# Holding later batches' attention behind the MLP tiles, and moving the first loads to a second DMA queue

## The chip, the cores and the metric

The kernel runs on one core of one Trainium2 chip. The metric is the device time of one execution in microseconds. One execution was taken by the hardware profiler; all times inside the kernel come from that one. The engines are TensorE (PE, with PEld for its weight loads), VectorE (DVE), ScalarE (ACT), GpSimd (POOL) and SyncE (SP), which issues DMAs. Each engine works through its own instructions in the order in which the program has them, and waits at the head of its queue.

## The reference

Eight batches of 512 tokens `x` and 32 state rows `state`, 8 heads of 64. Attention runs both ways between them, and every row of the result passes an MLP with a squared ReLU:

```python
scores  = scale * x @ state.T        # per batch and head
xread   = softmax(scores)  @ state   # 512 rows
sread   = softmax(scale * state @ x.T) @ x   # 32 rows
attn    = concat([xread, sread])     # 8 * 544 = 4352 rows of 512
h       = attn @ w_in                # 512 -> 2048
out     = (relu(h) ** 2) @ w_out     # 2048 -> 512
```

`w_in` and `w_out` come as 64-bit floats.

## The kernel before

**Arithmetic.** Most products are made from a high and a low part (`split`, L96: ScalarE rounds to the high part at L97, VectorE or GpSimd subtracts it at L98 for the low part). So one product is three matmuls: high by high, low by high, high by low. The 64-bit weights arrive as pairs of 32-bit words and `singles` (L100) turns them into 32-bit floats: one ScalarE operation (L108) and three VectorE operations (L109, L113, L117).

**z.** The token rows never get `xread` as such. The state of each head is multiplied into `w_in` first, which gives z (`z_part`, L148, products pz), written to DRAM as `zd` and fetched for each batch by `z_fetch`. zs[0] serves batches 0 to 3, zs[1] batches 4 to 7. `z_state` (L127) loads and splits the state for it.

**Attention of a batch** (`attention`, `attention_group`, two groups p and q of four heads). Steps: `pad` (L242, loads a batch's state as sp_raw), `load_t` (x transposed, xt_raw), `cut_t` (split), `scores` (pst in batches 0 and 1; two halves pq added into st from batch 2 on), `soft1` and `soft1b` (the softmax over the state rows: L315 maximum, L316 subtraction, L317 exponential, L322 sum, L324 reciprocal, L325 product, L327 transpose into `at`, then split into a_hi and a_lo). The subtraction and the product run on GpSimd in batches 0 to 2. The state's own reads come three batches later: `load_n`, `cut_n` (xn_hl), `turn` (L338 to L340 scale e, then transposes pt into e_hl) and `read` (products pr).

**MLP tiles** (`mlp`, L372). A tile is one batch with 128 of the 2048 hidden columns. `up` makes ph from z and a (L392, six matmuls), then relu (L394, ScalarE), square (L396 on ScalarE for the first ten tiles, L398 on VectorE afterwards) and the split into g_hi and g_lo. `down` (L418, twelve matmuls into four po) follows two tiles later. The tiles run in this order: batch 0 with column blocks 0 to 5, batch 1 with 0 to 9, batch 0 with 6 to 15, batch 1 with 10 to 15, then batches 2 to 7 with all sixteen each. So batch 1 starts with the seventh tile, and batch 2 with tile 32 counted from 0. After a batch's last block, L599 adds po to the sums.

**What sets the order.** `mlp` calls `aux` twice for each tile, a slot each. `aux` asks two lists of class `Ahead` for steps: `weights` (loading and converting w_in and w_out, making z) and `reads` (attention of batches 1 and on, and the reads). Each list spreads its steps evenly up to a due slot, and holds a step back until its `begin`. For batch b's attention the list is due one slot ahead of the batch's first tile; from batch 2 on it begins when batch b − 2 has ended: slot 52 for batch 2, due at slot 63. That is the order in which the program writes its instructions. Behind it a scheduler orders each engine's instructions by a timing model of its own and by dependencies, and may pull an instruction far ahead of where it was written.

Loads of weights, and some others, share four buffers (tag `raw`), and are freed by the conversion. The loads were all issued by SP; the stores of z (`zd`, L217) by ScalarE.

Of the kernel before, what the change touches and what calls it, by code (L numbers as in the profile page):

```python
# [9 lines left out]
F32 = mybir.dt.float32  # L10
# [8 lines left out]
def memory_attention_then_relu2_ffn(  # L19
# [71 lines left out]
    zd, st, z_first = {}, {}, []  # L91
# [2 lines left out]
            zd[G, k] = dr.tile([P, NG, HG, FW], F32, name=f"zd_{G}_{k}")  # L94

    def split(hi, lo, src, eng_lo):  # L96
        nc.scalar.copy(out=hi, in_=src)  # L97
        eng_lo.tensor_sub(out=lo, in0=src, in1=hi.bitcast(F32))  # L98

    def singles(out_f, words):  # L100

        low, high = words[..., 0], words[..., 1]
        bits = out_f.bitcast(I32)
        nc.scalar.activation(out_f, high.bitcast(F32), AF.Abs, scale=2.0**-112)  # L108
        nc.vector.tensor_scalar(  # L109
            out=bits, in0=bits, scalar1=3, scalar2=0x7FFFFFF8,  # L110
            op0=ALU.logical_shift_left, op1=ALU.bitwise_and,
        )
        nc.vector.scalar_tensor_tensor(  # L113
            out=bits, in0=high, scalar=-0x80000000, in1=bits,
            op0=ALU.bitwise_and, op1=ALU.bitwise_or,
        )
        nc.vector.scalar_tensor_tensor(  # L117
            out=bits, in0=low, scalar=29, in1=bits,
            op0=ALU.logical_shift_right, op1=ALU.bitwise_or,
        )  # L120


    def z_state(G):
        if G == 0:
            raw = sb.tile([P, H, GB * N], F32, name="st_f", tag="x_hl", bufs=1)
            st["raw"] = raw
        else:  # L127
            raw = sb.tile([P, H, GB * N], F32, name="st_raw", tag="raw", bufs=RAW)
        for j in range(2):
            nc.sync.dma_start(out=raw[j * D:(j + 1) * D].rearrange("d h m -> d (h m)"), in_=stT[G])  # L130
        hi = sb.tile([P, H, GB * N], F32R, name="stz_hi", bufs=1)
        lo = sb.tile([P, H, GB * N], F32R, name="stz_lo", bufs=1)
        if G:
            split(hi, lo, raw, nc.gpsimd)
        else:
            for i in range(2):
                own = slice(i * D, (i + 1) * D)
                other = slice((1 - i) * D, (2 - i) * D)
                for v in (hi, lo):
                    nc.gpsimd.memset(v[other, i::2, :].bitcast(F32), 0.0)  # L140
                split(hi[own, i::2, :], lo[own, i::2, :], raw[own, i::2, :], nc.vector)
        st[G] = hi, lo

    def z_part(G, k, g):
# [5 lines left out]
        def load():  # L150
            if G:
                box["wf"] = sb.tile([P, nq, FW], F32, name="wf", bufs=2)
                nc.sync.dma_start(out=box["wf"], in_=wd[k][:, ccs, :])
                return
            raw = sb.tile([P, nq, FW, 2], I32, name="w_raw", tag="raw", bufs=RAW)
            nc.sync.dma_start(out=raw.rearrange("p c f w -> p (c f w)"), in_=w_in[k * NG + g])
            box["raw"] = raw

        def convert():
            wf = sb.tile([P, nq, FW], F32, name="wf", bufs=2)  # L160
            singles(wf, box["raw"])
            nc.sync.dma_start(out=wd[k][:, ccs, :], in_=wf)
            box["wf"] = wf

# [52 lines left out]
                nc.scalar.dma_start(out=dst, in_=stage)  # L217
            return run

        return load, convert, cut, [product(i) for i in range(2)]  # L220

    def z_fetch(b, k):
        if k or b:
# [157 lines left out]
    def mlp(width, fcs, first, rows, aux):  # L381
# [6 lines left out]
        def up(fc):  # L388
# [10 lines left out]
            units[0] += 1  # L399
            hi = sb.tile([P, S], F32R, name="g_hi", bufs=2)[:, :width]  # L400
            lo = sb.tile([P, S], F32R, name="g_lo", bufs=2)[:, :width]
            split(hi, lo, ph, nc.vector)
            gs[fc] = hi, lo

        def down(i):
# [65 lines left out]
    def emit(step):  # L471
        step()
        emitted[step] = slot[0]

    class Ahead:

        def __init__(self):
            self.steps, self.due, self.done = [], [], 0  # L480

        def add(self, steps, due, begin=0):
            self.steps += [(begin, s_) for s_ in steps]
# [23 lines left out]
    for b in range(B):
        for g in range(NG):
# [169 lines left out]
```

## Time and profile before

| | us |
|---|---|
| three timed runs, median (lowest to highest) | 708.6 (707.11 to 710.06) |
| the profiled execution's own time | 708.43 |
| its span, first to last instruction | 706.6 |
| mean granted TensorE clock | 0.973 of full speed |
| TensorE busy | 669.8 |
| VectorE busy | 452.2 |
| ScalarE busy | 398.3 |
| GpSimd busy | 199.3 |

The profile has several views. The page gives busy shares, forty slices of the span in tenths, and the chain of work that ended last. A table of stretches gives each engine's busy time in a stretch, the granted clock and the DMA share. Groups of instructions by line give count, busy time and mean duration, and what ended the idle time before them. The timeline gives single instructions with their start, duration and, in brackets, the idle time of the engine before them and its releaser. Names like po<-wo_hi,g_hi say what is written from what. Matmuls are pipelined, so the distance between two starts is the time that one takes from the engine, not its shown duration.

### The profile page before, as it was taken

The numbers are of one execution on the slowest core, as the hardware profiler recorded it, in microseconds if no ns is written. First come the engines' busy times: TensorE is split into PE (matmuls) and PEld (weight loads), VectorE is DVE, ScalarE is ACT, GpSimd is POOL, SyncE is SP. The second block draws the span as 40 slices with busy tenths as digits, with TensorE's granted clock in tenths as the row PEclk, the third lists the DMA queues.
The fourth block names the chain that finished last, engine by engine and source line by source line (L and its number), as shares of the span: only waits on it lengthen the run. The fifth ranks groups of instructions, "written<-read, shape, count | busy, mean of one in ns | idle before, by whom it ended". The sixth has DMA issues, their size and how long they took to land.

```text
span 706.6 us, 9753 instructions
## 1 busy us (share of the span) xinstructions
PE 669.8 (95%) x3152; PEld 551.6 (78%) x3152; DVE 452.2 (64%) x757; ACT 398.3 (56%) x727; POOL 199.3 (28%) x181
## 2 busy tenths in 40 slices
PE   4688789999999999999999999999999999999997
PEld 2355668778888888888888878888888888888996
DVE  4859999758456944447945794797944445443553
ACT  3767687567565863467735653665654344332442
POOL 2314433345443540053403240344242022000000
PEclk8589999999999999999999999999999999999999
DMA  8898899435363542344423312412241112100421
GB/s 276 270 315 283 258 306 315 131 97 153 98 202 122 166 149 62 102 135 120 135 78 120 87 48 74 139 58 90 89 150 61 30 31 90 31 16 0 130 80 32
DMA packets 74548, 90.58 MB, mean 128 GB/s; under 512 B 7680, under 2 KB 57600, under 8 KB 74496
## 3 DMA queue, kind: packets, MB, share of 16 engines
q1 hardware_dynamic: 56896, 72.90, 32.9%
q10 hardware_dynamic: 17600, 17.04, 7.1%
q8 instruction: 25, 0.41, 0.3%
q14 instruction: 27, 0.22, 0.1%
HBM read 60.03 MB, written 29.88 MB: 127 GB/s over the span
## 4 chain that ended last, share of the span: by engine, by line
PE 79%; DVE 8%; DMA 6%; issue 2%; ACT 2%; SPq 1%; POOL 0%; DVEq 0%; ACTq 0%; POOLq 0%
PE po L418 47%; PE ph L392 25%; PE pz L203 3%; DMA wo_raw<-w_out 2%; PE pr L355 2%; DMA sp_raw<-stP 2%; PE pq L288 1%; PE pt L343 1%; DVE wf L117 1%; DVE wf L113 1%; DVE z_lo L98 1%; DVE g_lo L98 1%; DMA zd<-z_stage 1%; DMA xt_raw<-xT 1%; DVE wf L109 1%
## 5 line engine op out<-in xcount | busy, mean ns | idle before, releaser
L418 PE MATMUL po<-wo_hi,g_hi 128*128 128x512 f32 x544 | 217.3, 400 | 0.6 <-ACT g_hi L97 0.5
L418 PE MATMUL po<-wo_lo,g_hi 128*128 128x512 f32 x544 | 215.0, 395 | 0.0
L398 DVE TENSOR_TENSOR ph<-ph,r 128x512 f32<-128x512 f32 (+1 forms) x134 | 89.1, 665 | 169.1 <-ACT r L394 168.9
L394 ACT ACTIVATE r<-ph 128x512 f32<-128x512 f32 (+1 forms) x144 | 82.1, 572 | 171.0 <-PE ph L392 169.6
L418 PE MATMUL po<-wo_hi,g_lo 128*128 128x512 f32 x544 | 152.2, 392 | 0.0
L418 PEld LDWEIGHTS po<-wo_hi,g_hi 128*128 128x128 f32 x544 | 103.9, 191 | 22.4 <-ACT g_hi L97 2.0
L418 PEld LDWEIGHTS po<-wo_lo,g_hi 128*128 128x128 f32 x544 | 103.9, 191 | 19.5
L418 PEld LDWEIGHTS po<-wo_hi,g_lo 128*128 128x128 f32 x544 | 101.5, 189 | 21.1 <-issue 1.0
L98 DVE TENSOR_TENSOR g_lo<-ph,g_hi 128x512 fp32r<-128x512 f32 (+1 forms) x144 | 94.4, 656 | 36.3 <-ACT g_hi L97 27.7
L97 ACT CAST g_hi<-ph 128x512 fp32r<-128x512 f32 (+1 forms) x144 | 81.0, 563 | 57.9 <-DVE ph L398 51.7
L392 PE MATMUL ph<-a_hi,z_hi 128*128 128x512 f32 x256 | 81.4, 399 | 2.6 <-DVE nm L306 1.5
L392 PE MATMUL ph<-a_lo,z_hi 128*128 128x512 f32 x256 | 80.1, 392 | 0.0
L392 PE MATMUL ph<-a_hi,z_lo 128*128 128x512 f32 x256 | 80.0, 394 | 0.0
L98 POOL TENSOR_TENSOR xn_hl<-xn_raw,xn_hl 128x1024 fp32r<-128x1024 f32 x16 | 38.9, 2432 | 138.0 <-ACT xn_hl L97 71.2
L182 POOL TENSOR_TENSOR w<-wf,w 64x512 fp32r<-64x512 f32 x32 | 43.0, 1343 | 74.9 <-ACT w L181 69.8
L392 PEld LDWEIGHTS ph<-a_hi,z_hi 128*128 128x128 f32 x256 | 47.6, 190 | 15.2 <-DVE g_lo L98 2.1
L392 PEld LDWEIGHTS ph<-a_hi,z_lo 128*128 128x128 f32 x256 | 48.5, 190 | 10.4
L392 PEld LDWEIGHTS ph<-a_lo,z_hi 128*128 128x128 f32 x256 | 48.2, 189 | 10.5 <-issue 0.3
L98 POOL TENSOR_TENSOR xt_hl<-xt_raw,xt_hl 128x1024 fp32r<-128x1024 f32 x12 | 28.9, 2406 | 75.4 <-ACT xt_hl L97 43.7
L98 DVE TENSOR_TENSOR z_lo<-z_raw,z_hi 128x512 fp32r<-128x512 f32 x64 | 47.9, 750 | 0.3 <-DMA wd<-wf 0.3
L97 ACT CAST z_hi<-z_raw 128x512 fp32r<-128x512 f32 x64 | 39.2, 615 | 1.3 <-DMA wd<-wf 0.8
L98 POOL TENSOR_TENSOR wo_lo<-wof,wo_hi 128x512 fp32r<-128x512 f32 x16 | 25.2, 1578 | 51.4 <-ACT wo_hi L97 51.4
(97 smaller groups left out, 833.7 us busy)
## 6 DMA issues: line engine op xcount, KB each, us to landing
zd<-z_stage ACTq DMA_DIRECT2D x64, 256.0 KB, 3.2
z_raw<-zd SPq DMA_DIRECT2D x252, 64.0 KB, 2.4
xt_raw<-xT SPq DMA_DIRECT2D x16, 512.0 KB, 3.8
w_raw<-w_in SPq DMA_DIRECT2D x16, 512.0 KB, 5.3
wo_raw<-w_out SPq DMA_DIRECT2D x16, 512.0 KB, 5.8
xn_raw<-xn SPq DMA_DIRECT2D x16, 512.0 KB, 3.9
out<-sum SPq DMA_DIRECT2D x32, 256.0 KB, 2.5
wd<-wf SPq DMA_DIRECT2D x16, 256.0 KB, 3.7
```

Source lines behind the costliest of these rows:

```text
L97: nc.scalar.copy(out=hi, in_=src)
L98: eng_lo.tensor_sub(out=lo, in0=src, in1=hi.bitcast(F32))
L109: nc.vector.tensor_scalar(out=bits, in0=bits, scalar1=3, scalar2=0x7FFFFFF8, op0=ALU.logical_shift_left, op1=ALU.bitwise_and,)
L113: nc.vector.scalar_tensor_tensor(out=bits, in0=high, scalar=-0x80000000, in1=bits, op0=ALU.bitwise_and, op1=ALU.bitwise_or,)
L117: nc.vector.scalar_tensor_tensor(out=bits, in0=low, scalar=29, in1=bits, op0=ALU.logical_shift_right, op1=ALU.bitwise_or,)
L182: nc.gpsimd.tensor_sub(out=w[other], in0=wf[own], in1=w[own].bitcast(F32))
L203: nc.tensor.matmul(pz[:, q, :], lhsT=a[:, h, :], rhs=w, start=j == 0, stop=j == len(todo) - 1,)
L355: nc.tensor.matmul(pr[:, q].rearrange("p i c -> p (i c)"), lhsT=my["e"][:, t, q].rearrange("p i n -> p (i n)"), rhs=my["xn"][:, t, q].rear ...
L392: nc.tensor.matmul(ph, lhsT=w, rhs=v, start=i == 0, stop=i == len(todo) - 1)
L394: nc.scalar.activation(r, ph, AF.Relu)
L398: nc.vector.tensor_mul(out=ph, in0=ph, in1=r)
L418: nc.tensor.matmul(po[t], lhsT=g, rhs=w, start=i == 0 and j == 0, stop=i == last and j == 2)
```

## The change

Four things change.

1. `mark` remembers, for each engine, the last of certain instructions: the two of the split of each tile's g, and the loads of weights on SP. The list `reads` is made with `behind=True`: each of its steps is written inside `behind_marks`, which forbids the scheduler to put any of the step's instructions on an engine ahead of that engine's remembered instruction. TensorE and GpSimd have no mark. The list `weights` stays free.
2. The first two halves of `w_in` (k = 0) are requested from ScalarE's queue instead of SP's.
3. The state's load for zs[0] goes to ScalarE's queue too, and each half of the partitions loads only the heads that it uses (half the bytes). Loading and splitting are two steps now, and the splitting is held behind the conversion of the second half of w_in.
4. `stT` keeps its dimension of heads on the way in. Arithmetic and amounts of work are otherwise the same.

```diff
+    def mark(*those):
+        for i in those:
+            marks[i.ins.engine] = i.ins
+
+    def behind_marks():
+        stack = ExitStack()
+        for i in marks.values():
+            stack.enter_context(tc.issue_after(i))
+        return stack
...
         for j in range(2):
-            nc.sync.dma_start(out=raw[j * D:(j + 1) * D].rearrange("d h m -> d (h m)"), in_=stT[G])
+            rows = slice(j * D, (j + 1) * D)
+            if G:
+                nc.sync.dma_start(out=raw[rows], in_=stT[G])
+            else:
+                nc.scalar.dma_start(out=raw[rows, j::2, :], in_=stT[G, :, j::2, :])
...
-            nc.sync.dma_start(out=raw.rearrange("p c f w -> p (c f w)"), in_=w_in[k * NG + g])
+
+            queue = nc.scalar if k == 0 else nc.sync
+            load = queue.dma_start(out=raw.rearrange("p c f w -> p (c f w)"), in_=w_in[k * NG + g])
+            if k:
+                mark(load)
...
-            split(hi, lo, ph, nc.vector)
+            mark(*split(hi, lo, ph, nc.vector))
...
         def next(self):
-            emit(self.steps[self.done][1])
+            with behind_marks() if self.behind else ExitStack():
+                emit(self.steps[self.done][1])
...
-        q["cut_t"], q["scores"], q["soft1"], p["soft1b"], q["soft1b"], lambda: z_state(0),
+        q["cut_t"], q["scores"], q["soft1"], p["soft1b"], q["soft1b"], lambda: z_state_load(0),
...
-    weights, reads = Ahead(), Ahead()
+    with tc.issue_after(z0[1][4]["done"].ins):
+        z_state_cut(0)
+
+    weights, reads = Ahead(), Ahead(behind=True)
```

The load in `wo_load` is marked as well. The orders of the engines move as follows. First VectorE just ahead of the seventh tile's g_lo, in the kernel before:

```order
L98 TENSOR_TENSOR w_1_865<-wf,w_0_864 128x512
L113 SCALAR_TENSOR_TENSOR wf<-w_raw,wf 128x512
L109 TENSOR_SCALAR wof<-wof 128x512
L117 SCALAR_TENSOR_TENSOR wf<-w_raw,wf 128x512
L113 SCALAR_TENSOR_TENSOR wof<-wo_raw,wof 128x512
L117 SCALAR_TENSOR_TENSOR wof<-wo_raw,wof 128x512
L98 TENSOR_TENSOR z_lo<-z_raw,z_hi 128x512
L98 TENSOR_TENSOR w_1_985<-wf,w_0_984 128x512
L109 TENSOR_SCALAR wf<-wf 128x512
L113 SCALAR_TENSOR_TENSOR wf<-w_raw,wf 128x512
L117 SCALAR_TENSOR_TENSOR wf<-w_raw,wf 128x512
L98 TENSOR_TENSOR g_lo<-ph,g_hi 128x512
```

and in the changed kernel (wf is a half block of w_in, wof a block of w_out, w_1 the low part of a wf for z):

```order
L98 TENSOR_TENSOR w_1_1267<-wf,w_0_1266 128x512
L127 SCALAR_TENSOR_TENSOR wf<-w_raw,wf 128x512
L98 TENSOR_TENSOR z_lo<-z_raw,z_hi 128x512
L131 SCALAR_TENSOR_TENSOR wf<-w_raw,wf 128x512
L123 TENSOR_SCALAR wof<-wof 128x512
L127 SCALAR_TENSOR_TENSOR wof<-wo_raw,wof 128x512
L131 SCALAR_TENSOR_TENSOR wof<-wo_raw,wof 128x512
L98 TENSOR_TENSOR w_1_1359<-wf,w_0_1358 128x512
L98 TENSOR_TENSOR g_lo<-ph,g_hi 128x512
```

The last low part of w_in ahead of the seventh g_lo was w_1_985; now two later halves (1113 and 1267) and the last, 1359, stand ahead of it, with more conversions of w_out.

Then TensorE where batch 2 begins. ph_1944 is the up product of its first tile, a_hi_1686 its attention; po0_1759 to po3_1762 are batch 1's sums. Before:

```order
L418 MATMUL po3_1762<-wo_hi7_1383,g_lo_1849 128x512
L392 MATMUL ph_1944<-a_hi_1686,z_hi_1950 128x512 x2
L392 MATMUL ph_1944<-a_hi_1686,z_lo_1951 128x512 x2
L392 MATMUL ph_1944<-a_lo_1687,z_hi_1950 128x512 x2
L288 MATMUL pq_2331<-xt_hl_2276,sp_hl_77 128x512
L203 MATMUL pz_2357<-w2_0_2291,stz_lo_1971 128x256
L418 MATMUL po0_1759<-wo_hi7_1383,g_hi_1887 128x512
L418 MATMUL po0_1759<-wo_lo7_1384,g_hi_1887 128x512
```

Now:

```order
L448 MATMUL po2_1761<-wo_hi7_1383,g_lo_1888 128x512
L448 MATMUL po3_1762<-wo_hi7_1383,g_lo_1888 128x512
L422 MATMUL ph_1944<-a_hi_1686,z_hi_1950 128x512
L422 MATMUL ph_1989<-a_hi_1686,z_hi_1950 128x512
L422 MATMUL ph_1944<-a_hi_1686,z_hi_1950 128x512
L422 MATMUL ph_1944<-a_hi_1686,z_lo_1951 128x512 x2
L422 MATMUL ph_1944<-a_lo_1687,z_hi_1950 128x512
L422 MATMUL ph_1989<-a_hi_1686,z_hi_1950 128x512
L422 MATMUL ph_1989<-a_hi_1686,z_lo_1951 128x512 x2
L422 MATMUL ph_1989<-a_lo_1687,z_hi_1950 128x512
```

The up product stood ahead of the down products of batch 1's last tile (g_hi_1887); now it stands behind all of them, and the first two tiles' ups stand together.

Last, ScalarE at the same place in the changed kernel; q1_1821 is the softmax of batch 2's second group, at_1857 and at_1896 the transposed results of its first and second group:

```order
L323 COPY st_low_1818<-pq_1815 64x512
L97 CAST g_hi_1887<-ph_1877 128x512
L245 COPY z_stage_2008<-pz_2003 128x512
L211 CAST w2_0_2112<-wf_2025 64x512
L245 COPY z_stage_2016<-pz_2011 128x512
L211 CAST w2_1_2113<-wf_2025 64x512
L247 DMA zd_1_0_99<-z_stage_2008 128x2x256
L339 ACTIVATE e2_1826,s2_1827<-st_1808,nm2_1823 128x512
L97 CAST a_hi_1686<-at_1857 128x512
L347 ACTIVATE q1_1821<-q1_1821 128x512
L247 DMA zd_1_0_99<-z_stage_2016 128x2x256
L97 CAST a_hi_1686<-at_1896 128x512
```

and before, where the exponential of q1_1821 stood among earlier tiles (g_hi_1473 is of one of them):

```order
L215 COPY z_stage_2016<-pz_2011 128x512
L181 CAST w2_1_2113<-wf_2025 64x512
L217 DMA zd_1_0_99<-z_stage_2008 128x2x256
L309 ACTIVATE e2_1826,s2_1827<-st_1808,nm2_1823 128x512
L97 CAST g_hi_1473<-ph_1463 128x512
L217 DMA zd_1_0_99<-z_stage_2016 128x2x256
L317 ACTIVATE q1_1821<-q1_1821 128x512
L394 ACTIVATE r_1525<-ph_1509 128x512
```

The exponential and the second a_hi now stand directly ahead of batch 2's first tile, behind two z_stage, two w, one e and the first a_hi.

More of the change, by code (lines that the diff above doesn't have):

```diff
@@ L96, in split @@
     def split(hi, lo, src, eng_lo):
-        nc.scalar.copy(out=hi, in_=src)
-        eng_lo.tensor_sub(out=lo, in0=src, in1=hi.bitcast(F32))
+        a = nc.scalar.copy(out=hi, in_=src)
+        return a, eng_lo.tensor_sub(out=lo, in0=src, in1=hi.bitcast(F32))
+    marks = {}
+    def mark(*those):
[6 more added lines that the diff above has]
+        return stack
     def singles(out_f, words):
@@ L116, in singles @@
         )
-        nc.vector.scalar_tensor_tensor(
+        return nc.vector.scalar_tensor_tensor(
             out=bits, in0=low, scalar=29, in1=bits,
@@ L123, in z_state, with z_state_load @@
     def z_state(G):
+        z_state_load(G)
+        z_state_cut(G)
+    def z_state_load(G):
         if G == 0:
@@ L129, in z_state, with z_state_cut @@
         for j in range(2):
-            nc.sync.dma_start(out=raw[j * D:(j + 1) * D].rearrange("d h m -> d (h m)"), in_=stT[G])
+            rows = slice(j * D, (j + 1) * D)
[3 more added lines that the diff above has]
+                nc.scalar.dma_start(out=raw[rows, j::2, :], in_=stT[G, :, j::2, :])
+        st["raw", G] = raw
+    def z_state_cut(G):
+        raw = st["raw", G]
         hi = sb.tile([P, H, GB * N], F32R, name="stz_hi", bufs=1)
@@ L160, in convert @@
             wf = sb.tile([P, nq, FW], F32, name="wf", bufs=2)
-            singles(wf, box["raw"])
+            box["done"] = singles(wf, box["raw"])
             nc.sync.dma_start(out=wd[k][:, ccs, :], in_=wf)
@@ L218, in product @@
             return run
-        return load, convert, cut, [product(i) for i in range(2)]
+        return load, convert, cut, [product(i) for i in range(2)], box
     def z_fetch(b, k):
@@ L443, in wo_load @@
         raw = sb.tile([P, DM, 2], I32, name="wo_raw", tag="raw", bufs=RAW)
-        nc.sync.dma_start(
+        mark(nc.sync.dma_start(
             out=raw.rearrange("p e w -> p (e w)"), in_=w_out[fc * P:(fc + 1) * P, :]
-        )
+        ))
         wf = sb.tile([P, DM], F32, name="wof", bufs=2)
@@ L475, in memory_attention_then_relu2_ffn, with __init__ @@
     class Ahead:
-        def __init__(self):
-            self.steps, self.due, self.done = [], [], 0
+        def __init__(self, behind=False):
+            self.steps, self.due, self.done, self.behind = [], [], 0, behind
         def add(self, steps, due, begin=0):
@@ L504, in memory_attention_then_relu2_ffn @@
     lags = {}
-    for _, _, c, ps in zs[0] + zs[1]:
+    for _, _, c, ps, _ in zs[0] + zs[1]:
         lags[ps[0]] = [(c, 2)]
@@ L657 @@
             state.reshape(B * N // 128, 128 // N, H, N, D).transpose(0, 4, 2, 1, 3)
-        ).reshape(B * N // 128, D, H * 128),
+        ),
         "stP": np.ascontiguousarray(
```

## Prediction

> **What bounds the kernel now.** I read the page's busy shares and its forty slices first, then a table of stretches, then TensorE's waits in the first 125 us.
>
> ```profile
> PE 669.8 (95%) x3152; PEld 551.6 (78%) x3152; DVE 452.2 (64%) x757; ACT 398.3 (56%) x727; POOL 199.3 (28%) x181
> ...
> PE   4688789999999999999999999999999999999997
> ...
> PEclk8589999999999999999999999999999999999999
> ```
>
> ```profile
> 0.00:30.00 30.00, 13.77 (x35) 6.91 (x36) 17.95 (x38) 17.18 (x37) 9.91 (x18) 0.72 0.86 278
> 30.00:60.00 30.00, 24.28 (x84) 16.74 (x84) 22.43 (x39) 18.90 (x37) 8.13 (x6) 0.82 0.84 272
> 60.00:101.40 41.40, 33.74 (x154) 26.67 (x153) 39.65 (x63) 31.59 (x60) 17.56 (x11) 0.88 0.88 296
> 101.40:140.00 38.60, 38.03 (x179) 31.48 (x179) 34.45 (x51) 26.77 (x48) 12.27 (x9) 0.99 0.73 231
> 140.00:212.00 72.00, 71.25 (x345) 59.77 (x344) 44.31 (x76) 46.59 (x83) 35.81 (x30) 1.00 0.46 140
> ```
>
> The columns of the table are the stretch, its length, the busy time of PE, PEld, DVE, ACT and POOL, the granted clock, the DMA share and GB/s. TensorE sets the end: from slice 7 on it is full. It idles 30.00 − 13.77 = 16.2, 5.7 and 7.7 us in the first three stretches, 29.6 us by 101.4, and 0.6 + 0.75 us in the next 110 us. So all that a reordering can win lies ahead of 101.4 us, and any idle put behind that point is lost time in full, since no engine is behind TensorE there. In the third stretch VectorE is busy 39.65 of 41.40 us: it, with the DMA queues at 0.88, paces the conversion of the weights. TensorE waits for that:
>
> ```profile
> PE pz L191 <- DVE wf L117: 11.7, 4, 4.0
> ```
>
> 101.4 us is where the seventh MLP tile, batch 1's first, starts its down product; VectorE's g_lo of the same tile starts then:
>
> ```profile
> 101.39 0.63 PE L418 MATMUL po<-wo_hi,g_hi 128*128 128x512 f32 x1
> ```
> ```profile
> 101.87 0.68 DVE L98 TENSOR_TENSOR g_lo<-ph,g_hi 128x512 fp32r<-128x512 f32 x1
> ```
>
> **The change: the ramp up to the seventh tile.** Attention of batch 1 is still due at the same tile, but its steps now stand behind the tile whose slot emits them, while conversions of later weights may still run ahead. Counted in VectorE's two orders up to the seventh g_lo, the new one holds two more halves of w_in (16 against 14), three more rows of w_out (12 against 9) and three more cuts w, and lacks four scalings e with their two short operations and two cuts sp_hl, all moved behind. Their prices, as groups of the first 125 us:
>
> ```profile
> L113 DVE SCALAR_TENSOR_TENSOR wf<-w_raw,wf 128x512 int32<-128x512 int32 x16 | 13.2, 825 | 0.2
> L117 DVE SCALAR_TENSOR_TENSOR wf<-w_raw,wf 128x512 int32<-128x512 int32 x16 | 13.2, 822 | 0.2
> L113 DVE SCALAR_TENSOR_TENSOR wof<-wo_raw,wof 128x512 int32<-128x512 int32 x14 | 10.6, 756 | 0.1
> L117 DVE SCALAR_TENSOR_TENSOR wof<-wo_raw,wof 128x512 int32<-128x512 int32 x14 | 10.5, 751 | 0.1
> L109 DVE TENSOR_SCALAR wf<-wf 128x512 int32<-128x512 int32 x16 | 10.2, 637 | 9.3 <-ACT wf L108 9.3
> L98 DVE TENSOR_TENSOR w<-wf,w 128x512 fp32r<-128x512 f32 x10 | 8.7, 870 | 1.6 <-ACT w L97 1.6
> L109 DVE TENSOR_SCALAR wof<-wof 128x512 int32<-128x512 int32 x15 | 8.6, 570 | 6.2 <-ACT wof L108 6.2
> ...
> L340 DVE TENSOR_SCALAR e<-e,s 128x512 f32<-128x512 f32 x4 | 3.7, 930 | 0.0
> ...
> L98 DVE TENSOR_TENSOR sp_hl<-sp_raw,sp_hl 64x128 fp32r<-64x128 f32 x2 | 1.3, 650 | 0.0
> ...
> L338 DVE TENSOR_SCALAR s<-s 128x1 f32<-128x1 f32 x4 | 0.6, 146 | 0.4 <-ACT e L309 0.4
> ...
> L339 DVE RECIPROCAL s<-s 128x1 f32<-128x1 f32 x4 | 0.6, 140 | 0.0
> ```
>
> Added: 2 × (0.64 + 0.83 + 0.82) + 3 × (0.57 + 0.76 + 0.75) + 3 × 0.87 = 4.6 + 6.2 + 2.6 = 13.4 us. Taken away: 4 × (0.93 + 0.15 + 0.14) + 1.3 = 6.2 us. VectorE reaches the seventh g_lo 7.2 us of work later.
>
> Against this stands what VectorE no longer waits for: 9.3 us ahead of its first operation, and 6.2 us twice for rows of w_out. Both go back to DMA:
>
> ```profile
> 5.00:10.00 5.00, 5.00 (x6) 2.08 (x7) 0.74 (x2) 0.67 (x1) 0.00 (x0) 1.00 1.01 306
> ```
> ```profile
> 4.93 6.09 PE L298 MATMUL pst<-xt_raw,sp_f 128*128 128x512 f32 x8 [4.93 <-DMA xt_raw<-xT]
> ...
> 8.57 0.67 ACT L108 ACTIVATE wf<-w_raw 128x512 f32<-128x512 f32 x1 [3.90 <-DMA w_raw<-w_in]
> ```
>
> The queues are full (1.01 of their time) from 5 us. The first weights, landed at 8.57 us behind 1 MB of x, now stand in a second queue beside that x. If they landed as the first x does now, 3.6 us would be won; if x takes the same time from them, nothing or, since b = 0's softmax then starts later, less than nothing. I take 1 us, nearer to the full queue. Batch 1's x (1 MB, 3.4 us at 306 GB/s) and half of the state's 512 KB no longer stand ahead of the first rows of w_out; of the 6.2 us I take 2 us, because the same megabyte now falls among later rows. Together 3 us, between −2 and 8.
>
> The Trainium skill (DMA: Bandwidth & Descriptors, Issuing engines are not separate DMA queues) says that transfers started by different engines run on the same 16 DMA engines and interleave, and that issuing from several saves only the issuing time. By that rule the 1 us is nil and the sum below is 1 us higher; the share of 1.01 agrees with it.
>
> TensorE also does 24 more products pz ahead of the seventh tile in the new order (132 against 108), which are then not behind it. Two rows of its timeline, six starts apart, price one:
>
> ```profile
> 201.44 0.28 PE L203 MATMUL pz<-w,stz_lo 128*128 128x256 f32 x1
> ...
> 202.15 0.28 PE L203 MATMUL pz<-w,stz_lo 128*128 128x256 f32 x1
> ```
>
> (202.15 − 201.44) / 6 = 0.118 us, 2.8 us in all. And of the 1.3 us idle and the 0.4 us at clock 0.99 in the 110 us behind, half may go with the lighter VectorE: 0.9 us. The ramp costs 7.2 − 3 − 2.8 − 0.9 = 0.5 us, between −4.5 (8 won by earlier data) and 5.5 (2 lost).
>
> **The change: the start of batch 2.** Batch 2's attention may begin only at tile 26 and is due at tile 32. Until now the scheduler ran it far ahead: in TensorE's order its last scores pq stand some 200 rows ahead of its first up product. Now 32 rows lie between, and its second a_hi behind batch 1's last sum. What TensorE still has after the last pq is 24 down products and 8 pz:
>
> ```profile
> 213.32 0.39 PE L418 MATMUL po<-wo_hi,g_hi 128*128 128x512 f32 x1
> ...
> 214.23 1.07 PE L418 MATMUL po<-wo_hi,g_lo 128*128 128x512 f32 x4
> ```
>
> (214.23 − 213.32) / 4 = 0.23 us, so 24 × 0.227 + 8 × 0.118 = 6.4 us of cover. The chain that must run in it, as groups from 125 to 235 us (the ends of each engine's kind stand for the others of the same size, which lie between):
>
> ```profile
> L293 ACT COPY st_low<-pq 64x512 f32<-64x512 f32 x8 | 4.6, 582 | 1.3 <-PE pq L288 1.2
> ...
> L309 ACT ACTIVATE e<-st,nm 128x512 f32<-128x512 f32 x3 | 2.2, 726 | 0.1
> L316 POOL TENSOR_TENSOR q<-q,m 128x512 f32<-128x512 f32 x2 | 2.1, 1056 | 1.9 <-DVE nm L306 1.9
> ...
> L305 DVE TENSOR_REDUCE nm<-st 128x1 f32<-128x512 f32 x3 | 1.9, 644 | 0.0
> L317 ACT ACTIVATE q<-q 128x512 f32<-128x512 f32 x3 | 1.9, 635 | 0.2 <-DVE q L316 0.2
> ...
> L327 DVE STREAM_TRANSPOSE at<-q 128x512 f32<-128x512 f32 x2 | 1.4, 711 | 1.3 <-POOL q L325 1.3
> ```
>
> By dependencies alone: two st_low (1.2), six full-width VectorE operations and a g_lo between them (7 × 0.68 = 4.8), two on GpSimd (2.1), the exponential and a_hi (1.25), two short ones (0.4): 9.75 us, so 3.3 us are uncovered. But ScalarE's new order puts two z_stage, two w, the exponential e and the first a_hi ahead of the exponential of q. The first z_stage waits for a pz behind 20 of the 24 down products (5.0 us); six operations of 0.6 to 0.73 us follow, so the exponential starts at about 9.0 us instead of 5.6. That makes 13.2 us, 6.8 us past the cover; two half products of the group already cut fill 0.45 us of them: 6.4 us.
>
> Then the tiles' pipeline is empty. TensorE has issued both ups and must wait for relu, square and g_hi of the first, with a second relu and a z_hi between on ScalarE: about 4 × 0.6 us less one matmul, 2.2 us. Idle: 8.6 us, between 3.3 − 0.45 + 2.2 = 5.0 and, with a tenth of a microsecond for each of some fourteen handovers, 10.
>
> An idle TensorE is also clocked down afterwards:
>
> ```profile
> 59.53 0.39 PE L203 MATMUL pz<-w,stz_lo 128*128 128x256 f32 x1 [2.38 <-ACT e L309]
> ```
> ```profile
> 60.00:70.00 10.00, 9.93 (x37) 6.81 (x35) 8.36 (x14) 7.72 (x14) 5.10 (x3) 0.83 0.93 343
> ```
>
> A gap of 2.38 us was followed by ten microseconds at a granted 0.83: 1.7 us lost. I add 1.7 once. The start of batch 2 costs 8.6 + 1.7 = 10.3 us.
>
> **Small places.** At the start of batch 7 the new order sets the second half of the first up product (a_lo) behind all down products of batch 6, so the same relu, square, g_hi (2.4 us, a second relu ahead) has 1.4 us of the next up and 0.9 us of eight pr as cover, counting 0.118 for a pr as for a pz of the same size. With handovers 0.9 us idle, between 0 and 2. The other starts (3 to 6) keep an up product one tile ahead, as before: nothing. The reads of batch 0 and the scalings of e fall in stretches where VectorE is busy 44.31 of 72.00 us: nothing, and 2 us at worst if one of them blocks a g_lo. Issuing four loads from ScalarE, early, where it waits for data anyway: nothing.
>
> **Sum.** The profiled execution took 708.43 us, 0.17 below the median of the three runs (708.6). 708.43 + 0.5 + 10.3 + 0.9 = 720.1 us.
>
> **The rivals.** *The ramp pays and the boundary is covered.* TensorE has 29.6 us of idle to win; if the waits of 9.3 and 6.2 us mostly go (8 us) the ramp ends 4.5 us earlier, and if batch 2's chain runs early by as much, so that only 1 us is seen, the time is 708.43 − 4.5 + 1 = 704.9 us, 704 with nothing seen. It decides where VectorE's seventh g_lo comes before about 101 us. For it speaks that the queues are full early; against it that the two chains both hang on TensorE's own order, which moves with it, so an earlier ramp does not widen the cover of 6.4 us. *A short gap.* ScalarE gets through earlier than I think and only the dependencies count: 5.0 us and a ramp at −2: 711.4, or 713 with a clock spell. Here the skill bears: TensorE: Matmul & The Clock Gate (Part 1: The HAM clock gate) has the half clock set in after an idle window of about 3.4 us, so the lower figure would hold if the 5 us fall into two pieces; the row of 2.38 us speaks for the higher one. *The ramp pays, the boundary stalls.* 708.43 − 4.5 + 10.3 + 0.9 = 715.1 us. *The change does nothing*: the orders of all engines differ, so I give this no chance.
>
> **Chances and range.** The forecast 0.50, the ramp that pays with a stall 0.15, the short gap 0.22 (half of it within 0.5%), the covered boundary 0.13. About 0.5% (3.5 us, so 705.1 to 712.1) is what a measurement of this kernel can tell from no change. Faster 0.13, same 0.11, slower 0.50 + 0.15 + 0.11 = 0.76. Top of the range: a ramp at 5.5 and a boundary of 11.7 give 726.5; the low end takes in the short gap and leaves the covered boundary out: 707. Range 707 to 727.
>
> **What would show it.** Right: VectorE's first operation before 8.5 us; the seventh g_lo at 105 to 109 us; near 205 to 220 us an idle of 5 to 8 us of TensorE ahead of an up product that waits for a_hi, a second one of some 2 us for g_hi, and a clock under 0.9 in the ten microseconds behind; nothing of either in 140 to 700 us otherwise but 1 us near the start of batch 7. Wrong: TensorE full from 140 to 230 us, or fewer than 25 us of idle before the seventh tile.

## The result, and the profile after

The changed kernel takes 727.75 us (median of four runs, 725.2 to 728.14) against 709.18 us before (four runs, 707.11 to 710.06): 1.026 times as long, interval 1.0225 to 1.0292. The forecast was 720.1 us, 707 to 727. The direction was right, the size was not: 18.6 us were lost where 11.5 were forecast. The profiled execution took 725.2 us, its span is 723.4 us, 16.8 more than before.

The table of stretches of the changed kernel, with the columns of the one before (length, busy PE, PEld, DVE, ACT and POOL, granted clock, DMA share, GB/s):

```profile
0.00:30.00 30.00, 13.97 (x43) 7.53 (x44) 19.92 (x35) 17.02 (x35) 10.78 (x18) 0.83 0.72 252
30.00:60.00 30.00, 21.79 (x72) 15.27 (x72) 22.11 (x32) 17.14 (x33) 6.92 (x5) 0.77 0.92 308
60.00:101.40 41.40, 32.86 (x148) 26.79 (x149) 38.93 (x63) 30.46 (x58) 17.31 (x12) 0.84 0.85 278
101.40:140.00 38.60, 33.72 (x163) 27.80 (x162) 30.14 (x41) 28.48 (x51) 15.92 (x11) 1.00 0.83 255
140.00:212.00 72.00, 72.00 (x319) 59.64 (x318) 35.59 (x57) 30.14 (x54) 5.86 (x3) 1.00 0.19 57
212.00:235.00 23.00, 15.21 (x60) 11.41 (x59) 14.36 (x29) 10.73 (x20) 9.77 (x8) 0.85 0.34 116
```

Up to 140 us TensorE idles 16.0 + 8.2 + 8.5 + 4.9 = 37.7 us; before it was 16.2 + 5.7 + 7.7 + 0.6 = 30.2. That is 7.5 us lost in the ramp, 2.5 of them from 30 to 60 us and 4.3 behind 101.4 us. The clock took the same from both: busy time times one less the clock, summed over these four stretches, is 12.6 us after and 12.7 before. From 140 to 212 us TensorE is now full, and from 212 to 235 us it idles 7.8 us where it was full before.

What TensorE waited for from 200 us on, as single rows of its timeline:

```profile
211.85 1.07 PE L318 MATMUL pq<-xt_hl,sp_hl 128*128 128x512 f32 x4
...
218.25 1.09 PE L448 MATMUL po<-wo_hi,g_lo 128*128 128x512 f32 x4
221.59 0.73 PE L422 MATMUL ph<-a_hi,z_hi 128*128 128x512 f32 x2 [2.25 <-ACT a_hi L97]
226.12 0.79 PE L422 MATMUL ph<-a_hi,z_hi 128*128 128x512 f32 x1 [3.80 <-ACT a_hi L97]
...
232.50 0.50 PE L448 MATMUL po<-wo_hi,g_hi 128*128 128x512 f32 x1 [1.74 <-ACT g_hi L97]
...
389.16 0.50 PE L448 MATMUL po<-wo_hi,g_hi 128*128 128x512 f32 x1 [1.68 <-ACT g_hi L97]
...
604.69 0.50 PE L448 MATMUL po<-wo_hi,g_hi 128*128 128x512 f32 x1 [0.93 <-ACT g_hi L97]
```

This is the gap at the start of batch 2: after the last scores pq at 211.85 and 6.4 us more work, 2.25 us and 3.80 us for batch 2's two a_hi, then 1.74 us for the first g_hi, since no finished tile is left whose down product could run. ScalarE at the same place:

```profile
217.97 0.59 ACT L245 COPY z_stage<-pz 128x512 f32<-128x512 f32 x1 [3.37 <-PE pz L233]
...
220.21 0.72 ACT L339 ACTIVATE e<-st,nm 128x512 f32<-128x512 f32 x1
...
221.44 0.63 ACT L347 ACTIVATE q<-q 128x512 f32<-128x512 f32 x1
225.45 0.62 ACT L97 CAST a_hi<-at 128x512 fp32r<-128x512 f32 x1 [3.39 <-DVE at L357]
```

The exponential of q waits in its queue behind z_stage, w, e and the first a_hi, and starts at 221.44. The clock there, again as stretches:

```profile
221.60:222.30 0.70, 0.70 (x2) 0.28 (x2) 0.20 (x1) 0.47 (x1) 0.62 (x2) 1.00 1.03 378
...
226.10:228.50 2.40, 2.38 (x6) 1.90 (x7) 0.00 (x0) 0.00 (x0) 1.28 (x1) 0.50 0.00 0
228.50:230.80 2.30, 2.26 (x6) 1.24 (x4) 0.00 (x0) 0.43 (x1) 0.00 (x0) 0.50 0.00 0
```

After 2.25 us of idle the clock was still 1.00, after 3.80 us more it was 0.50 for both up products: (2.38 + 2.26) × 0.5 = 2.3 us lost. In all the place costs 7.8 + 2.3 = 10.1 us.

In the ramp, the start of VectorE, the first scores, and the seventh g_lo:

```profile
6.94 0.43 DVE L123 TENSOR_SCALAR wf<-wf 128x512 int32<-128x512 int32 x1 [6.94 <-ACT wf L122]
```
```profile
7.51 1.19 PE L328 MATMUL pst<-xt_raw,sp_f 128*128 128x512 f32 x1 [7.51 <-DMA xt_raw<-xT]
```
```profile
110.33 0.68 DVE L98 TENSOR_TENSOR g_lo<-ph,g_hi 128x512 fp32r<-128x512 f32 x1
```

The first weights come 2.3 us earlier than before (6.94 against 9.26), x comes 2.6 us later (7.51 against 4.93), and the seventh g_lo 8.5 us later (110.33 against 101.87).

### The profile page after: what moved, and what is told of

The parts are those of the page before. It is cut to its first block, busy times and chain, and to the rows that moved or that the text cites. A ratio compares the mean times of both kernels' runs of the same rounds, so it can differ in the third digit from the quotient of the medians.

```text
span 723.4 us, 9780 instructions
## 1 busy us (share of the span) xinstructions
PE 670.3 (93%) x3152; PEld 553.8 (77%) x3152; DVE 455.6 (63%) x757; ACT 398.5 (55%) x727; POOL 199.7 (28%) x181
## 4 chain that ended last, share of the span: by engine, by line
PE 83%; DMA 7%; ACT 5%; issue 2%; DVE 1%; SPq 1%; POOL 0%; ACTq 0%; DVEq 0%; POOLq 0%
PE po L448 50%; PE ph L422 26%; DMA wo_raw<-w_out 2%; PE pz L233 2%; PE pr L385 2%; DMA zd<-z_stage 2%; PE pq L318 2%; DMA st_f<-stT 1%; PE pt L373 1%; ACT z_stage L245 1%; DMA w_raw<-w_in 1%; ACT g_hi L97 1%; ACT r L424 0%; DMA sp_raw<-stP 0%; ACT wf L122 0%
## 5 line engine op out<-in xcount | busy, mean ns | idle before, releaser
L448 PE MATMUL po<-wo_hi,g_lo 128*128 128x512 f32 x544 | 155.0, 394 | 0.0
L422 PE MATMUL ph<-a_hi,z_hi 128*128 128x512 f32 x256 | 83.2, 404 | 8.3 <-ACT a_hi L97 6.9
L422 PE MATMUL ph<-a_lo,z_hi 128*128 128x512 f32 x256 | 82.3, 397 | 0.0
L422 PE MATMUL ph<-a_hi,z_lo 128*128 128x512 f32 x256 | 82.3, 401 | 0.0
L98 POOL TENSOR_TENSOR xt_hl<-xt_raw,xt_hl 128x1024 fp32r<-128x1024 f32 x12 | 28.9, 2405 | 110.9 <-ACT xt_hl L97 92.5
L98 DVE TENSOR_TENSOR z_lo<-z_raw,z_hi 128x512 fp32r<-128x512 f32 x64 | 50.3, 787 | 0.6 <-ACT z_hi L97 0.6
L245 ACT COPY z_stage<-pz 128x512 f32<-128x512 f32 x64 | 37.4, 585 | 17.2 <-PE pz L233 14.0
L98 POOL TENSOR_TENSOR a_lo<-at,a_hi 128x512 fp32r<-128x512 f32 x16 | 22.5, 1407 | 67.2 <-ACT a_hi L97 67.0
```

Source lines behind the costliest of these rows:

```text
L98: return a, eng_lo.tensor_sub(out=lo, in0=src, in1=hi.bitcast(F32))
L245: nc.scalar.copy(out=stage, in_=pz)
L422: nc.tensor.matmul(ph, lhsT=w, rhs=v, start=i == 0, stop=i == len(todo) - 1)
L448: nc.tensor.matmul(po[t], lhsT=g, rhs=w, start=i == 0 and j == 0, stop=i == last and j == 2)
```

## Experiments

All kernels were timed in five rounds, beside the kernel before on the same chip, whose median was 707.8 to 708.4 us. No experiment leaves out or changes any of the computation. Theory A is the forecast's with the ramp corrected: the marks make the whole loss, in two separate places, the gap ahead of batch 2 and the ramp. Its rival B puts the ramp's loss on the moved requests; the others (C to M) are told where they are tested. Most kernels free the steps of one batch from the marks; each step then carries a flag:

```diff
-            with behind_marks() if self.behind else ExitStack():
+            with behind_marks() if self.steps[self.done][2] else ExitStack():
...
-            reads.add(steps, 2 * begins[b] - 1, 2 * ends[b - 2] if b > 1 else 0)
+            reads.add(steps, 2 * begins[b] - 1, 2 * ends[b - 2] if b > 1 else 0, held)
```

**The requests alone, the marks alone.** The first has `Ahead(), Ahead()`, so nothing is held. The second has all loads as in the kernel before, and the marks.

> Only the requests are moved (first halves of w_in and the state's halves on ScalarE's queue, its cut held); no step of attention is held behind tiles. Theory A (the marks make the whole loss): 709 us, within 2 of the kernel before; x lands some 2.5 us later and the first weights 2.3 us earlier, which cancel. Theory B (the second queue delays x, and that delay is the ramp's loss): 712 to 714 us, TensorE's idle before the seventh tile up by 3 or more.

Measured: 706.06 us, 0.997 of before (0.9957 to 0.9982).

> Only the marks: all loads from SyncE's queue as in the kernel before. Theory A: 726 to 729 us, as slow as the full change. Theory B: 721 to 724 us, since x again lands at 5 us and the ramp loses less.

Measured: 727.96 us, 1.0292 (1.0274 to 1.0311). The marks make the whole loss. Theory B falls: x was late in the first kernel too, at 7.55 us, and it was no slower.

**One batch free.** `held` is `b != 2`, then `b != 1`, then `b > 2`.

> The full change, but the steps of batch 2's attention are free again; those of batch 1 and of batches 3 on are held. Theory A: the gap ahead of batch 2 (7.8 us idle and about 2.3 us at a low clock) goes, the ramp's loss stays: 717 to 719 us. Rival C (VectorE is the real bound from 100 to 240 us, so that the wait comes back elsewhere): above 723 us with an idle of 5 us or more somewhere between 110 and 240 us.

Measured: 719.21 us, 1.0163 (1.0146 to 1.018). The gap is gone, and with it the 8.5 us; there is no idle from 140 to 400 us, and the time is below C's 723, so C falls. Ahead of 140 us TensorE idles 41.5 us, though, 3.8 more than in the full change.

> The full change, but the steps of batch 1's attention are free again; those of batches 2 on are held. Up to the seventh g_lo VectorE has 42 operations for w_in and 30 for w_out, against 48 and 36 with all held. Theory A: the gap ahead of batch 2 stays at 7.5 to 8.5 us idle, the ramp's loss of 5 to 7 us mostly goes: 720 to 723 us. Theory B: the ramp's loss stays, since it is the requests': 726 to 728 us.

Measured: 713.51 us, 1.008 (1.0063 to 1.0096): more than theory A gave. The gap of batch 2 stands in it unchanged, in TensorE's timeline:

```profile
212.00 0.50 PE L422 MATMUL ph<-a_hi,z_hi 128*128 128x512 f32 x1 [2.25 <-ACT a_hi L97]
...
216.52 0.79 PE L422 MATMUL ph<-a_hi,z_hi 128*128 128x512 f32 x1 [3.79 <-ACT a_hi L97]
...
222.90 0.50 PE L448 MATMUL po<-wo_hi,g_hi 128*128 128x512 f32 x1 [1.74 <-ACT g_hi L97]
```

> The full change, with the steps of batch 1's and batch 2's attention both free; batches 3 on and all reads behind them are held. Theory A (the two holds are separate costs): 713.5 us with batch 1 free, less the gap ahead of batch 2 (7.8 us idle and 2.3 us at a low clock) gives 703.4 us, below the kernel with the requests alone (706.1 us). Rival E (batch 2's attention, once free, takes VectorE's time in the ramp, as the 719.2 us with batch 2 alone free suggest): 706 to 709 us, with 3 us or more of TensorE's idle between 101 and 140 us.

Measured: 704.93 us, 0.9949 (0.9931 to 0.9966), with 0.9 us of idle between 101 and 140 us: theory A. TensorE is full where the gap was:

```profile
212.00:235.00 23.00, 23.00 (x115) 19.40 (x114) 15.19 (x27) 13.21 (x24) 7.79 (x5) 1.00 0.40 129
```

The four kernels make a square:

| us | batch 2 free | batch 2 held |
|---|---|---|
| batch 1 free | 704.93 | 713.51 |
| batch 1 held | 719.21 | 727.75 |

Holding batch 2 costs 8.6 or 8.5 us, holding batch 1 costs 14.3 or 14.2 us, and the rest of the change gains some 3.3 us on the kernel before. The costs add up, so they are two separate ones. That they agree to a tenth is luck, for the four kernels were not timed side by side: taken from the ratios to the kernel before (0.9949, 1.008, 1.0163 and 1.0259, of 708 us), batch 2 costs 9.3 or 6.8 us and batch 1 15.2 or 12.7.

**A wider cover for batch 2.** `2 * begins[b] - (6 if b == 2 else 1)` as the due slot.

> The full change with all steps held, but batch 2's attention is due five slots earlier. In TensorE's order 24 down products, 6 of an up product and 5 pz lie between its last scores and its first up product (7.4 us of cover against 6.4), and that up product stands ahead of the last downs of batch 1. Theory A (the gap is the chain less the cover): 3 to 6 us idle there instead of 7.8, 722 to 726 us. Rival C (the gap is set by something else, such as ScalarE's z_stage alone): unchanged within 1 us, 727 to 729 us.

Measured: 722.29 us, 1.02 (1.0174 to 1.0226), and in TensorE's timeline:

```profile
227.00 0.80 PE L422 MATMUL ph<-a_hi,z_hi 128*128 128x512 f32 x1 [2.94 <-ACT a_hi L97]
...
233.38 0.79 PE L448 MATMUL po<-wo_hi,g_hi 128*128 128x512 f32 x1 [1.74 <-ACT g_hi L97]
```

4.7 us of idle instead of 7.8. From the product behind the last scores to the one that waits for the second a_hi it takes 14.1 us now, 13.4 in the full change, and TensorE has 11.1 us of work in it against 7.3: 3.8 − 0.7 = 3.1 us less idle. So the gap is the chain less its cover, though the cover grew by more than the expected 1.0 us. The same hold, due earlier, costs less; the 5.5 us won in time are more than the 3.1 here, and the idle of 1.68 us near 389 us is gone as well.

**What of batch 1's hold costs.** `behind_marks` takes only the marks of loads (SyncE), then only those of the cuts (ScalarE, VectorE), for `b == 1`.

> The full change, but batch 1's attention is held on SyncE alone (its loads stand behind the weights' loads that were already requested), and free on ScalarE and VectorE. VectorE has 43 operations for w_in, 30 for w_out and 8 cuts w ahead of the seventh g_lo. Theory D (the order of the conversions on VectorE is what holding batch 1 costs): 1.6 us of VectorE more than with batch 1 free, 714 to 716 us. Rival L (the order of the loads is the cost): 722 to 728 us.

Measured: 719.62 us, 1.0162 (1.0139 to 1.0185), 6.1 above batch 1 free.

> The full change, but batch 1's attention is held on ScalarE and VectorE alone (behind the split of the last tile's g), and its loads are free on SyncE. VectorE has 45 operations for w_in, 32 for w_out and 8 cuts w ahead of the seventh g_lo. Theory D: 3 operations for w_in, 2 for w_out and a cut w more than with batch 1 free, 4.5 us of VectorE: 717 to 720 us. Rival L (the order of the loads is the cost): 713 to 715 us. Rival F (any hold on these two engines costs the whole): 726 to 728 us.

Measured: 724.77 us, 1.022 (1.0197 to 1.0243), 11.3 above. Each hold alone costs more than theory D's count of VectorE's work gives, and together (14.2) less than their sum. None of the theories fits either run: 719.62 lies between D and L, 724.77 between D and F.

**VectorE's work taken away.** `split(w2[0], w2[1], wf, nc.gpsimd)` instead of `nc.vector`, in the full change and with batches 1 and 2 free.

> The full change, but the low parts w of w_in for the first z are subtracted by GpSimd and no longer by VectorE: ten operations of 0.87 us fewer on VectorE ahead of the seventh g_lo (132 operations against 142), the same products in nearly the same order on TensorE. Theory D (VectorE's work up to the seventh tile paces the ramp, and holding batch 1 costs because it puts more of it there): the seventh g_lo comes 4 to 9 us earlier than 110.3 and the time is 719 to 724 us. Rival G (the conversions are not what TensorE waits for; loads, ScalarE's order or the handover are): 726 us or more, since the product pz only changes whom it waits for.

Measured: 732.83 us, 1.0347 (1.0328 to 1.0365).

> The same move of the low parts w to GpSimd in the kernel with batches 1 and 2 free (704.9 us). VectorE has 120 operations ahead of the seventh g_lo against 128. Theory D: 700 to 704 us. Rival G: 705 us or more.

Measured: 708.96 us, 1.001 (0.9998 to 1.0022). Both lost 4 to 5 us, and both times are what rival G gave. But the move did not do what it was made for. A group of conversions on VectorE in the first 110 us, in the full change:

```profile
L127 DVE SCALAR_TENSOR_TENSOR wof<-wo_raw,wof 128x512 int32<-128x512 int32 x12 | 8.2, 684 | 0.2
L131 DVE SCALAR_TENSOR_TENSOR wof<-wo_raw,wof 128x512 int32<-128x512 int32 x12 | 8.2, 680 | 0.1
```

and with w on GpSimd:

```profile
L127 DVE SCALAR_TENSOR_TENSOR wof<-wo_raw,wof 128x512 int32<-128x512 int32 x11 | 8.9, 810 | 0.2
L131 DVE SCALAR_TENSOR_TENSOR wof<-wo_raw,wof 128x512 int32<-128x512 int32 x11 | 8.6, 779 | 0.1
```

The second number is the mean of one in ns: 779 to 810 instead of 680 to 684; some of them now run beside GpSimd (its rows are in the last section). Up to the seventh g_lo VectorE was busy 90.9 us with ten operations fewer, 89.8 with them, and that g_lo came at 112.8 us instead of 4 to 9 us earlier than 110.3. In the second kernel it was 85.7 against 83.6 us. So these two runs took no busy time from VectorE and test neither D nor G; they only show that GpSimd is no relief here.

**Smaller loads of the state, and marks for the late batches alone.** The first is the kernel before with each half's own heads, from SyncE; the second is the marks alone with `held` as `b > 2`.

> The kernel before with one edit: each half of the partitions loads only its own heads of the state, still requested by SyncE. 256 KB less among the first loads is 0.8 us at 306 GB/s: 707 to 708 us if the early DMA queue counts in full, 708 to 708.5 if other loads hide it; 706 if this edit alone is what the moved requests gained.

Measured: 705.11 us, 0.9961 (0.9947 to 0.9976): 3 us for 256 KB less, where full queues give 0.8.

> Only the marks, and only for batches 3 on and the reads behind them; batches 1 and 2 free, all requests as in the kernel before. If the moved requests (2.0 us) and these holds add up, the 704.9 us of the kernel with both becomes 706.5 to 707.5 us. If the reads of batch 0, which go out of the ramp with these holds, are what pays, 705 us; if the holds pay nothing, 708 to 709 us.

Measured: 703.59 us, 0.9937 (0.9921 to 0.9952), the fastest variant of the change, and below both kernels. The reads of batch 0, out of the ramp by these holds, are the likely gain, which no run tells alone; the moved requests add nothing to it (704.93 with them).

**DMA or VectorE in the ramp.** A second store of eight halves after `wd`, then three repeats of the last conversion step for four halves, both in the kernel before:

```diff
             nc.sync.dma_start(out=wd[k][:, ccs, :], in_=wf)
+            if G == 0 and 2 <= k * NG + g < 10:
+                more = dr.tile([P, nq, FW], F32, name=f"more_{k}_{g}")
+                nc.sync.dma_start(out=more, in_=wf)
```

> The kernel before, with the halves 2 to 9 of w_in stored to DRAM a second time (eight more stores of 256 KB in the ramp, 2.1 MB, 7 us of full DMA queues at 300 GB/s), nothing else. Theory M (the DMA queues pace the ramp): 713 to 716 us. Theories H and D (chains on the engines pace it, at a DMA share of 0.87): 708 to 711 us.

Measured: 702.95 us, 0.993 (0.9916 to 0.9945). More bytes did not cost; the kernel became 5.1 us faster, which no theory gave. The scheduler ordered the engines otherwise (three operations for w_in and two for w_out fewer on VectorE ahead of the seventh g_lo), and that is all that I can point to.

> The kernel before, with the last conversion step of the halves 4 to 7 of w_in done four times instead of once (the repeats change no bit): twelve more operations of 0.82 us on VectorE in the ramp, 9.8 us, no load more. Theories D and H (VectorE's queue paces the ramp): 714 to 718 us. Theory M: 708 to 710 us, since VectorE idles 21 us up to the seventh g_lo anyway.

Measured: 717.13 us, 1.0129 (1.0113 to 1.0146): 9.1 us for twelve operations, of which the groups of VectorE's first 110 us show

```profile
L165 DVE SCALAR_TENSOR_TENSOR wf<-w_raw,wf 128x512 int32<-128x512 int32 x12 | 9.7, 805 | 0.2
```

Theory M falls twice, and work added to VectorE's queue in the ramp is paid nearly in full although VectorE idles there. The repeats also hold their load buffers longer, which no run tells from the work itself.

**Both gains together.** The kernel with marks from batch 3 on, and the smaller loads.

> Marks for batches 3 on and the reads alone (703.6 us by itself), together with the smaller loads of the state (705.1 us by itself, 3.0 below the kernel before); all requests from SyncE. If both gains add up: 700 to 701.5 us. If both win the same idle time of the ramp: 703 to 704.5 us.

Measured: 706.46 us, 0.9975 (0.9962 to 0.9988): a smaller gain than either alone. Gains of 3 to 5 us in the ramp do not add up; each edit also reorders the rest, which is the likely reason.

**Batch 1 held, but due earlier.** `2 * begins[b] - (5 if b == 1 else 1)`.

> The full change, all steps held, but batch 1's attention is due four slots (two tiles) earlier: its last transpose stands behind 30 operations for w_in and 18 for w_out on VectorE, against 41 and 29. Theory H (the late end of batch 1's attention is what the hold costs): the second a_hi comes at 80 to 87 us instead of 96.3, and the time is 712 to 717 us, about that of the kernel with batch 1 free. Theories D and M (the hold costs by the work or the loads that it puts ahead): 721 us or more.

Measured: 718.35 us, 1.0162 (1.0142 to 1.0183), 9.4 below the full change, a little above the range of theory H. The second a_hi of batch 1 comes at 82.14 us, as expected. ScalarE's rows for it, before, after and here:

```profile
88.11 0.62 ACT L97 CAST a_hi<-at 128x512 fp32r<-128x512 f32 x1 [2.87 <-DVE at L327]
```
```profile
96.34 0.62 ACT L97 CAST a_hi<-at 128x512 fp32r<-128x512 f32 x1 [1.06 <-DVE at L357]
```
```profile
82.14 0.64 ACT L97 CAST a_hi<-at 128x512 fp32r<-128x512 f32 x1
```

4.8 us above the kernel with batch 1 free are left. TensorE's longest wait in this kernel is an early one. The full change has it too, and with batch 1 free it is shorter. TensorE's rows here, in the full change and with batch 1 free:

```profile
43.07 0.80 PE L448 MATMUL po<-wo_hi,g_hi 128*128 128x512 f32 x1 [9.10 <-ACT g_hi L97]
```
```profile
43.04 2.07 PE L221 MATMUL pz<-wf,st_f 64*128 64x256 f32 x4 [7.92 <-ACT z_stage L245]
```
```profile
39.26 2.07 PE L221 MATMUL pz<-wf,st_f 64*128 64x256 f32 x4 [3.68 <-ACT z_stage L245]
```

In the full change ScalarE, whose z_stage TensorE waits for, has itself stood for a row of w_out just before:

```profile
40.32 0.66 ACT L122 ACTIVATE wof<-wo_raw 128x512 f32<-128x512 f32 x1 [3.42 <-DMA wo_raw<-w_out]
```

In the kernel before, TensorE waits 2.66 us at that place. So the ramp loses time in a second place, 60 us ahead of the seventh tile. But this wait alone does not tell the time either: with batches 1 and 2 free it is 5.82 us, in a fast kernel.

The last run takes the hold of the loads away from this one.

> Batch 1's attention due four slots earlier, as in the run before it, and held on ScalarE and VectorE alone; its loads are free on SyncE. Its last transpose stands behind 30 operations for w_in and 19 for w_out on VectorE (30 and 18 with the loads held too). If the hold of the loads makes the remaining 4.85 us: 712 to 715 us, and TensorE's wait at 34 to 43 us falls from 9.1 to 5 us or less. If it does not: 717 to 720 us.

Measured: 719.45 us, 1.0171 (1.0155 to 1.0188), with a wait of 7.3 us there. The hold of the loads is not the rest. What the remaining 5 us are stays open. Nor does the seventh g_lo tell it: with the earlier due slot it comes at 97.0 us and in the last run at 92.5 us, sooner than the 98.2 with batch 1 free, and both kernels are slower.

The second a_hi of batch 1 beside the time, with the gap of batch 2 (8.5 us, where it stands in full) taken off in the last column:

| kernel | second a_hi at, us | time, us | without the gap |
|---|---|---|---|
| due earlier, cuts held | 80.4 | 719.5 | 711.0 |
| due earlier | 82.1 | 718.4 | 709.9 |
| w on GpSimd, batches 1, 2 free | 82.6 | 709.0 | 709.0 |
| marks from batch 3 on | 83.0 | 703.6 | 703.6 |
| marks from batch 3 on, smaller loads | 83.2 | 706.5 | 706.5 |
| requests alone | 84.5 | 706.1 | 706.1 |
| batches 1, 2 free | 84.9 | 704.9 | 704.9 |
| more stores | 85.4 | 703.0 | 703.0 |
| batch 1's loads held | 85.5 | 719.6 | 711.1 |
| smaller loads | 86.1 | 705.1 | 705.1 |
| batch 1 free | 86.5 | 713.5 | 705.0 |
| before | 88.1 | 708.1 | 708.1 |
| batch 1's cuts held | 89.1 | 724.8 | 716.3 |
| VectorE's work added | 96.2 | 717.1 | 717.1 |
| the full change | 96.3 | 727.75 | 719.2 |
| batch 2 due earlier | 99.3 | 722.3 | a smaller gap |
| marks alone | 99.4 | 728.0 | 719.5 |
| batch 2 free | 101.5 | 719.2 | 719.2 |
| w on GpSimd | 102.6 | 732.8 | a smaller gap |

A late a_hi goes with a slow kernel: from 96 us on, all are at 717 us or more. An early one does not make a fast kernel: between 80 and 90 us the times go from 703 to 716 us, and those slower than the kernel before are, with one exception, kernels that still hold something of batch 1.

## Why the prediction was right in one place and wrong in the other

**Batch 2's gap: right.** Forecast were 8.6 us idle and 1.7 us of clock, 10.3 in all; the trace has 7.8 and 2.3, 10.1, and the square of runs gives 8.5. The idle was 0.8 us smaller and the clock's share 0.6 larger, so the closeness of the two sums is in part luck. The exponential of q was put 9.0 us behind the last scores; 221.44 less 212.9, where they end, is 8.5. The forecast idle ahead of the up product (5 to 8 us) is 6.05, that for g_hi (about 2) is 1.74. That the gap is chain less cover was argued; the run with batch 2's earlier due slot bears it out.

**Batch 7: right.** 0.93 us at 604.69, forecast 0.9. The 1.68 us at 389.16, where batch 4 begins, were not forecast: the starts of batches 3 to 6 were put at nothing. The kernel before has 0.5 us of idle in that stretch of the program.

**The ramp: the term that was mis-sized.** It was +0.5 us, between −4.5 and 5.5. The trace shows 7.5 us more idle; in the medians, 18.6 less 8.5 for batch 2 and 2.1 for the two small places (1.68 + 0.93 − 0.5) leaves 8.0. The spans of the two profiled executions leave less, 16.8 − 10.1 − 2.1 = 4.6; the changed kernel's is the fastest of its four. The seventh g_lo was put at 105 to 109 us and came at 110.33. Taken piece by piece:

- VectorE's added work was 7.2 us. It was busy 89.8 us up to the seventh g_lo against 80.5, 9.3 more. The pieces were counted rightly, their durations came out 2 us longer in sum.
- "Together 3 us" were to come back from earlier data. VectorE idled 20.54 us up to the seventh g_lo against 21.36: 0.8 us. The first weights won 2.3 us and x lost 2.6. The prediction read the waits for rows of w_out as "6.2 us twice"; they are 6.2 us in all (2.06 at 37.09 and 4.10 at 50.32), and 5.9 us of such waits are there in the first 110 us of the changed kernel. The Trainium skill (DMA: Bandwidth & Descriptors, Issuing engines are not separate DMA queues) says that transfers of two engines share the same DMA engines; the two rows at 6.94 and 7.51 agree.
- 24 products more ahead of the tile were to give back 2.8 us. TensorE had been busy 73.6 us by then against 72.3: 1.3 us.
- Less idle behind it was to give 0.9 us; 1.3 us of before became 0.9, so 0.4.

9.3 − 0.8 − 1.3 − 0.4 = 6.8 us, where the forecast had 7.2 − 3 − 2.8 − 0.9 = 0.5. The count of the work was right, its price 2 us too low, and the three credits were each too large: all errors to one side. Only the first credit had bounds in the range; with none of the three the sum is 726.8 us. The rival in which the ramp pays fell for the change as a whole.

**What stood behind it.** The step looked at how much VectorE does up to a tile, not at what that tile waits for. Batch 1's first tile needs batch 1's attention, and its last transpose stands in VectorE's order behind 41 operations for w_in and 29 for w_out now, 34 and 21 before:

```profile
95.61 0.70 DVE L357 STREAM_TRANSPOSE at<-q 128x512 f32<-128x512 f32 x1
```

With the means of the three conversion steps that the prediction quotes, 7 × 0.76 + 8 × 0.69 = 10.8 us of work more stand ahead of it, and the a_hi made of it is 8.2 us later. TensorE's own wait for it is only 0.88 us (at 97.01), but the whole tile is late with it: its down product starts 13.7 us behind this a_hi (110.08), and in the kernel before 13.3 us. It is the same thing as at batch 2: the last steps of a held attention are written just ahead of the tile that needs them. This place was seen at batch 2 and not looked for at batch 1.

That holding batch 1 costs some 14 us is shown, and so is that its due slot makes 9.4 of them. That the slot acts through the late end of the chain is argued from the rows above, and it cannot be all: with only the loads or only the cuts held the second a_hi comes at 85.5 and 89.1 us, about where it is in the kernel before, and the holds cost 6.1 and 11.3 us even so. The other 5 us are not settled. Nor did the forecast see that the parts of the change that hold neither batch gain 3 to 4 us.

## What to carry to other kernels

A rule that keeps work from running ahead moves the last step of a held chain to the slot it is due in. So the due slot should lie a chain's length ahead of the use, and not one slot: earlier slots got back 5.5 of 8.5 us here and 9.4 of 14.2, and freeing the steps got back all. For each consumer in the change's reach, find the last link of the chain that feeds it in the new order and count what stands ahead of that, before counting an engine's total. Credits for waits that may vanish should be taken only where the row that ends the wait is itself moved.

## What the runs showed of the hardware

**VectorE beside GpSimd.** With w on GpSimd, a conversion that began just before GpSimd's subtraction took 0.69 us, one that began during it 1.67. VectorE's rows, then GpSimd's:

```profile
54.56 0.69 DVE L127 SCALAR_TENSOR_TENSOR wf<-w_raw,wf 128x512 int32<-128x512 int32 x1
55.28 1.67 DVE L131 SCALAR_TENSOR_TENSOR wf<-w_raw,wf 128x512 int32<-128x512 int32 x1
```
```profile
54.92 1.48 POOL L98 TENSOR_TENSOR w<-wf,w 128x512 fp32r<-128x512 f32 x1 [1.28 <-ACT w L97]
```

The operation that began at 55.28 ends 0.55 us after GpSimd's at 56.40. The Trainium skill (SBUF — State Buffer, SBUF: two separate sides) says that the two share a pair of ports under an exclusive lock, held for a whole instruction, when VectorE reads two operands from SBUF and GpSimd reads SBUF too; that is what these rows look like. So a subtraction moved from VectorE (0.81 us each) to GpSimd gave VectorE nothing back.

**The clock.** It falls to 0.50 some time after idling begins and comes back some time after work resumes. In the kernel before TensorE was full up to 57.1 us, idled 2.38 us and was full again from 59.5; the clock stayed at 1.00 up to 61.0 us and was 0.50 from there to 64.4. In the changed kernel it was 1.00 in the 0.7 us behind the 2.25 us of idle, fell to 0.50 at 224.4 us, within the 3.80 us, and was back at 231.2. What the 2.25 us alone would have done can't be seen. The Trainium skill (TensorE: Matmul & The Clock Gate, Part 1: The HAM clock gate) has the half clock set in after an idle window of about 3.4 us; the gap of 2.38 us is shorter and was followed by it even so.

**Bytes.** 2.1 MB more stores in a ramp whose DMA engines are busy 0.87 of the time (0.91 with them) did not show in the time, though the order of the work changed with them.
